# An attention and two-layer feed-forward chain on one core: the tokens of six batches in eight parts of 432 in place of twelve of 288

## The chip, the cores and the metric

The kernel runs on one core of a Trainium2 chip. The metric is the device time of one launch in microseconds (us). Three timed runs of the kernel before gave 1538.23, 1534.93 and 1534.53 us, so a median of 1534.93 us. Durations come from one profiled execution of its own, whose time was 1534.49 us; from its first to its last instruction that execution spans 1532.7 us.

## The reference

For each of 8 batches and 8 heads (576 tokens, 64 dimensions) the memories `phi` (576 x 32) are turned by a softmax over the tokens into weights `a`; `k_m` and `v_m` (32 x 64) are the sums of the keys and the values under these weights. The attention of a token is a softmax over its 32 scores, and its output is `attn @ v_m`:

```python
k_m = np.einsum('bhsm,bhsd->bhmd', a, k)
v_m = np.einsum('bhsm,bhsd->bhmd', a, v)
attn = softmax(q @ k_m.T / 8)
x = concat_heads(attn @ v_m)                  # 4608 x 512
x2 = np.square(np.maximum(x @ w_in, 0)) @ w_out      # 512 -> 2048 -> 512
h = x2 @ w_in2
out = (h - np.tanh(h)) @ w_out2
```

Inputs are drawn as float32; the weights arrive as float64 and are turned into float32 on the chip.

## The kernel before, in words

**Folding.** The first layer never sees `x`. For each batch `v_m` is multiplied into `w_in`: a tile `U` of a batch and a quarter of the hidden features (`fc` = 0 to 3, 512 features) is made by `u_make` (L327): 16 narrow matmuls (L336), two copies on ScalarE (L340) and two subtractions on VectorE (L341), which split U into a high and a low part. `w_in` is kept in memory as `w1_d` and read again for each batch from 2 on (`w1_load`, L190, 1 MB). The softmax over the 32 memories is transposed into `aT` (high and low part) by `att_b` (L360), one generator per half of a batch (288 tokens, `HT`). `att_a` (L217) makes `k_m` and `v_m`, one generator for four heads.

**Layer 1.** A part `u` is one half of a batch, so there are 16 parts (`NU`), and a step is one part and one tile `f` of 128 hidden features, so 256 steps. In a step, `l1_mm1` (L509) makes h by 6 matmuls (L519: three products of high and low, two halves of the 256 contracted rows), `l1_act` (L525) takes relu, square and a high part on ScalarE (L529, L530, L533) and the low part on GpSimd (L534), and `l1_mm2` (L537) adds into four banks of PSUM (512 columns each) by 12 matmuls (L546 to L548). Each of these 18 loads a fresh 128 x 128 weight tile and streams 288 columns. mm1 runs three steps ahead of mm2, act two. After its last step a part goes to memory as `x2_d` by four copies and four stores (`l1_out`, L554).

**Layer 2** (L628 to L698) takes blocks of 512 tokens: 12 matmuls for h, 12 for the output per step, each of 512 columns, 144 steps. Before the end of layer 1 its weights, split by `w2_conv` (L568) during layer 1, are loaded.

**Order.** The program is written out in the order in which generators advance. The opening is the list `ORDER` (L44): every word advances one generator (`i` att_a, `j` att_b, `u` u_make, `w` and `o` the weights' conversion), `S` is a step of layer 1 and `Z` four matmuls of a constant (`warm`, L503, L507; 8 instructions) that give TensorE something to do. A word whose generator is not ready is tried again later. After it, generators are set going at steps that formulas give (L760 to L772), and `tick` (L473) moves each of them by one stage per step when its resources, counted in `free` (L133), are there. Engines work through the program in order, so a matmul that waits holds up all that stand behind it on TensorE; SyncE does the same with the DMA issues.

**Places.** There are four tiles for U (`p_u`), two for `w_in` (`p_w`), two for `aT` (a whole batch each), two for raw weights (`p_raw`), and five of 640 elements in `p_g`; before, one of these five holds the high and the low part of a step (L531).

Of the kernel before, what the change touches and what calls it, by code (L numbers as in the profile page):

```python
# [32 lines left out]
NU = 2 * B  # L33
# [11 lines left out]
w00 w00 i01 w02 w00 w00 w00 o15 w13 o0 o1 w03 i00 i01 w10 w00 o1 w02 w12 w11 o0 Z i00 w03 o1 o1 w31 w11 i01 o0 o0 Z  # L45
i01 Z Z o8 w03 w10 w01 i01 o1 w02 o11 w03 S w10 S u01 w12 u02 j01 w13 Z i00 Z j01 i01 i00 o6 w20 j10 w01 i00 u02 i01
w01 i11 i01 i00 i00 i01 w03 u00 i00 i01 w02 w02 i00 o3 u02 w03 w20 i00 j01 j00 w20 o2 j00 w01 i01 w03 w02 o3 j00 w02
w10 j11 Z u00 w01 w11 u13 o5 o0 o0 w03 w11 w31 i01 u00 o3 j00 i01 o1 i01 o4 i10 u02 o14 w12 S o2 i00 j00 w13 j00 i00
w03 Z o8 j01 j00 j01 o1 j01 o0 o0 w01 o6 w00 j01 j00 Z w02 i00 w02 w02 i01 j00 w13 o3 w12 o2 o3 j00 S w20 o7 Z j01
j11 i10 u10 w32 o3 w33 j01 j00 u01 j01 Z o3 o1 Z i01 j00 Z Z Z o0 S u12 w12 o14 o3 S o0 w12 j01 o4 i00 o4 j00 o2 Z  # L50
w02 o0 o6 i01 w11 w01 o7 o7 o0 u10 j00 i01 j00 j01 w30 Z o5 w23 w02 o5 j10 w00 S w12 Z j00 j01 u03 o0 Z w03 i01 o11
j10 j00 w03 w21 w03 o3 j01 i11 u00 o10 i10 Z w10 w12 u00 w13 Z i00 w12 j01 o6 w11 u01 w03 Z Z o0 i11 i00 i00 w20 j00
j10 w10 j00 u02 w00 w03 i10 u01 o10 Z i11 w23 w13 Z o2 u11 j21 w00 w22 w10 w12 i10 o2 o5 o6 j10 j10 j00 j01 w12 o1
w32 w02 o0 o2 j10 Z w11 j01 u00 u02 o4 j20 w10 w12 o6 u02 w21 w13 w12 j01 o2 w32 i10 j01 i10 S o8 u01 o5 j01 j01 j10
w13 u02 o9 i10 u02 S o5 o1 u01 i10 o10 i10 o3 u02 o5 o1 o5 j01 j01 o1 u00 w12 o7 S o4 j11 o7 j01 i11 u13 j01 j01 u10
u00 u00 S o12 w02 o3 w20 u00 o7 o4 w23 j11 u10 w00 u13 w02 i00 w10 j01 u02 o7 w12 o7 o14 o5 u10 o4 i01 i11 o4 o11 w12
w10 w03 j10 w32 Z w33 j00 j10 w02 i10 o7 i20 u13 o15 w01 o1 i11 w10 o0 u00 u00 o13 i11 o11 w00 o6 o7 o0 w23 w23 i11
o5 o4 o6 o11 o4 i20 w00 o7 j00 j11 o9 o0 j00 w23 o6 w33 w30 o4 S o11 i20 o8 i11 i10 S o4 i01 w10 w21 i11 u03 o10 i11
j10 w10 i00 o3 i10 i11 w10 u02 w21 o6 j11 w20 j00 w11 w11 Z o3 w00 o8 j10 w00 i11 w00 o6 i00 u12 u03 w20 j10 u11 w22
S u13 o0 S j10 u10 j10 j11 o8 o11 S u11 w11 u03 o2 o3 j11 o10 o11 w10 o0 w12 u10 o13 j11 j21 u13 u01 o13 j11 o11 S S  # L60
u11 o8 S o11 w13 j20 j11 j00 w20 u00 u02 S i00 w10 S o13 w03 j11 i20 u11 u00 j11 o5 j11 w10 o7 o11 w20 o3 j20 w02 u00
w21 S o12 o7 i20 w03 o2 j10 o7 w33 w22 o9 j01 i10 u11 o8 u11 j20 S w23 j01 j20 w20 i20 S o11 i20 o2 w33 j20 j01 w00
o14 u02 w30 i20 u01 j21 i00 u10 o8 w32 w22 o9 w31 w31 o2 u02 S u02 i20 j01 w20 i20 w31 w30 S u00 u02 o14 w33 j01 w12
j01 j01 o3 S j01 S u01 w22 w31 o2 i20 u02 w33 w11 o3 o12 w33 w03 u11 w12 w21 w22 j11 j11 w11 o2 u00 w02 j01 w30 w30
w23 j11 j11 j10 j11 j21 o14 o13 o14 w23 S j20 w21 w30 w13 j11 w11 u11 w22 w31 w32 o0 i01 S w22 u12 w33 w33 w13 o5 u03
w00 w01 o11 w00 o4 w02 w21 w12 u00 S u12 w33 j11 w00 i01 w22 u01 w32 w30 w22 o14 u01 j21 j11 j00 o1 i01 u00 w13 w20 S
j21 S o1 o9 o1 w13 S o12 u03 S u10 u10 w13 o0 u10 w23 o14 w22 o9 i10 w22 o10 w22 w11 j11 w22 u12 u03 u12 u00 w20 o9
j21 w22 o13 o13
# [7 lines left out]
def moe_chain_kernel(ctx: ExitStack, tc: tile.TileContext, q, k, v, phi, w1i, w1o, w2i, w2o, out):  # L76
# [52 lines left out]

    def psum(p, name):  # L130
        return p.tile([P, 512], F32, tag=p.name, name=name)

    free = collections.Counter(af=2, b=2, f=3, raw=2, wo=FT, f2=3, kv=1, ph=1, q=1, e=1, vt=2, kt=2, qt=1, sm=1, at=2, w1=2, u=FC)  # L133
# [15 lines left out]
    def conv(src, out, p=None, ahead=1):  # L149
        yield "wo" if p else "raw"  # L150
        raw = slot(p or p_raw, [P, 512, 2], "raw", I32)
# [14 lines left out]
        give("wo" if p else "raw")  # L166
# [50 lines left out]
    def att_a(b, g):  # L217
# [3 lines left out]
        bank, w = (ps_a, "") if own else (ps_b, "b")  # L221

# [35 lines left out]
        for _ in range(4 if b > 2 else 1):  # L258
            yield
# [13 lines left out]
        yield w if own else "b e"  # L273
# [3 lines left out]
        e = e if own else slot(a_e, [P, NC, 4, M], f"e{b}_{g}")  # L277
# [4 lines left out]
        if not own:  # L282
            give("ph")
# [13 lines left out]
        give(*(["u"] * 2 if own else ["kv", "e"]))  # L297
        yield "-"
        n_d = 2 * D if dense else D
# [26 lines left out]

    def u_make(b, fc):  # L327
        yield lambda: {("a", b, g) for g in range(2)} | {("w", fc, pr) for pr in range(4)} <= done and (
            b < 2 or (b, fc) in w1) and (not fc or ("u", b, fc - 1) in done)
        yield "b b u"  # L330
# [7 lines left out]
        u = slot(p_u, [P, 2, 2, 512], f"u{b}_{fc}", F32R)  # L338
# [6 lines left out]
        if b < 2:  # L345
            w1_user(fc)
        else:
            give("w1")
# [6 lines left out]
    at = {}  # L355
# [4 lines left out]
    def att_b(b, r):  # L360
# [11 lines left out]
        elif r == 0:  # L372
            yield "q"
            qs[b] = slot(a_q, [P, 4, 2 * TB, 32], f"q{b}")
            for g in range(2):
                for dh in range(2):
                    src = q[b, 4 * g:4 * g + 4, :, 32 * dh:32 * dh + 32]
                    p0 = 64 * g + 32 * dh
                    nc.sync.dma_start(qs[b][p0:p0 + 32], src.rearrange("i (t p) d -> p i t d", p=32))
            for _ in range(4 if b > 2 else 1):  # L380
                yield
        yield lambda: b in qs
# [20 lines left out]
        yield "sm" if early else "b b" if b == 0 else "b b sm"  # L403
# [5 lines left out]
        give("qt")  # L409
        count(("sc", b), 2, "kt")  # L410
        yield "-"
        if (b, r) == (0, 1):
            s2, a = (slot(p_g, [P, 640], "smx")[:, :2 * HT] for _ in range(2))
        else:
            s2, a = (slot(a_sm, [P, 2 * HT], "sm") for _ in range(2))
# [21 lines left out]
        yield (lambda: b in at) if r else "at"  # L437
        if b not in at:
            at[b] = slot(p_at, [P, 2, 2, 2 * HT], f"aT{b}", F32R)
        hi, lo = (at[b][:, x, :, r * HT:(r + 1) * HT] for x in range(2))  # L440
# [3 lines left out]
        if (b, r) != (0, 1):  # L444
            give("sm")
        done.add(("b", b, r))
# [45 lines left out]
    x2_d = [p_d.tile([ET, P, HT], F32, name=f"x2_d{u}") for u in range(NU)]  # L492
# [16 lines left out]
    def l1_mm1(s):  # L509
# [27 lines left out]
    def l1_mm2(s):  # L537
# [5 lines left out]
        for e in range(ET):  # L543
            o = acc[u][e][:, :HT]
# [9 lines left out]
    def l1_out(u, a):  # L554
        outs = [slot(p_t, [P, HT], "xs") for _ in range(ET)]
        for e in range(ET):
            (nc.vector.tensor_copy if e % 2 and u > 3 else nc.scalar.copy)(outs[e], acc[u][e][:, :HT])  # L557
# [10 lines left out]
    def w2_conv(m, f):  # L568
# [26 lines left out]
    def x2_load(j, c, p_x2f):  # L595
# [8 lines left out]
        while c0 < 512 * (j + 1):  # L604
            u, o = divmod(c0, HT)
            n = min(HT - o, 512 * (j + 1) - c0)
# [153 lines left out]
    for b in range(2, B):  # L760
        s = 32 * (b - 1) - 20
        if b > 2:
            at_step(s, att_a(b, 0))
            at_step(s + 8, att_a(b, 1))
            at_step(s + 10, att_b(b, 0))
            at_step(s + 17, att_b(b, 1))
        for fc in range(FC):
            s0 = (45, 48, 60, 64)[fc] if b == 2 else 32 * (b - 1) + 20 + 4 * fc
            at_step(s0 - 8 if b > 2 else 34 + 2 * fc, w1_load(b, fc))
            at_step(s0, u_make(b, fc))  # L770
    for i in range(2 * FT):
        at_step(40 + 5.3 * i, w2_conv(i % 2, i // 2))  # L772
# [20 lines left out]
    for s in range(next_step[0], N1):  # L793
        if s == N1 - 22:
# [64 lines left out]
```

## Time and profile before

| | before |
|---|---|
| median of 3 runs | 1534.93 us |
| the profiled execution, its own time | 1534.49 us |
| its span | 1532.7 us |
| TensorE matmul busy, share of the span | 99% |
| TensorE weight load busy | 87% |
| VectorE, ScalarE, GpSimd busy | 65%, 55%, 37% |
| matmuls of layer 1's two products | 1536 and 3072 |

Read it so: TensorE's matmul row counts overlapping instructions, so its busy time says only that something is in flight. What a matmul costs is the distance from its start to the start of the next one. PEld is the weight load of TensorE, which runs beside matmuls.

### The profile page before, as it was taken

The page shows a single profiled execution, that of the slowest core. Times are in us where ns is not written, and L with a number is a line of the kernel's source. Part 1 is how long each engine was busy: PE and PEld are TensorE (multiplying, and loading weights), DVE is VectorE, ACT ScalarE, POOL GpSimd, SP SyncE. Part 2 cuts the span into 40 slices and gives each one's busy share as a digit, 9 for nine tenths or more (in the row PEclk, how much of TensorE's full clock was granted, in tenths as well). Part 3 has the DMA queues.
Part 4 walks back from the last instruction along what each step waited for, and adds up shares of the span by engine and source line. Part 5 has one row for each costly group of instructions (what it writes and reads, how often), then busy time and mean ns, then how long its engine had stood idle before and what let it go on. Part 6 is the DMA issues. An engine that isn't in the chain of part 4 may idle for free.

```text
span 1532.7 us, 25852 instructions
## 1 busy us (share of the span) xinstructions
PE 1519.9 (99%) x9880; PEld 1334.2 (87%) x9880; DVE 996.5 (65%) x1385; ACT 845.9 (55%) x1785; POOL 568.1 (37%) x530
## 2 busy tenths in 40 slices
PE   8999999999999999999999999999999999999998
PEld 7988999999899999999988888888888888888887
DVE  5966254545445434410488887878888787888886
ACT  4677676766666666655544444444444444444443
POOL 1565464525344342533442232423333242323322
PEclk7999999999999999999999999999999999999999
DMA  9885575766848383423630001010100101010000
GB/s 296 234 225 157 163 181 129 207 194 185 217 122 249 130 224 133 154 99 130 213 129 17 27 13 44 12 46 11 42 15 0 43 13 44 12 45 11 28 0 28
DMA packets 206907, 161.84 MB, mean 106 GB/s; under 512 B 142656, under 2 KB 182848, under 8 KB 203712
## 3 DMA queue, kind: packets, MB, share of 16 engines
q1 hardware_dynamic: 204336, 157.71, 34.3%
q0 software_dynamic: 2304, 2.36, 1.1%
q8 instruction: 77, 1.26, 0.3%
q14 instruction: 46, 0.38, 0.1%
q10 hardware_dynamic: 144, 0.13, 0.0%
HBM read 117.96 MB, written 42.21 MB: 105 GB/s over the span
## 4 chain that ended last, share of the span: by engine, by line
PE 85%; POOL 0%; ACT 0%; DVE 0%; issue 0%
PE h L637 26%; PE h L519 11%; PE o L683 9%; PE o L682 9%; PE o L681 9%; PE acc L548 7%; PE acc L547 7%; PE acc L546 7%; PE u L336 1%; PE vkm L293 1%; PE sc L408 0%; POOL g L534 0%; PE mb L275 0%; PE vkmT L311 0%; PE m1T L268 0%; ACT sm L427 0%
## 5 line engine op out<-in xcount | busy, mean ns | idle before, releaser
L637 PE MATMUL h<-x,wi 128*128 128x512 f32 x1728 | 414.6, 389 | 0.0
L667 POOL TENSOR_TENSOR gl<-pl,gh 128x512 fp32r<-128x512 f32 x144 | 187.9, 1305 | 535.7 <-PE o L682 512.4
L637 PEld LDWEIGHTS h<-x,wi 128*128 128x128 f32 x1728 | 324.2, 188 | 67.4 <-POOL x L617 0.2
L534 POOL TENSOR_TENSOR g<-gg,g 128x288 fp32r<-128x288 f32 x256 | 227.5, 905 | 358.9 <-ACT g L533 263.7
L649 ACT ACTIVATE u<-h 128x512 f32<-128x512 f32 x144 | 86.1, 598 | 417.5 <-PE h L637 417.5
L548 PE MATMUL acc<-g,wo 128*128 128x288 f32 x1024 | 301.4, 294 | 0.0
L547 PE MATMUL acc<-g,wo 128*128 128x288 f32 x1024 | 301.2, 294 | 0.1
L546 PE MATMUL acc<-g,wo 128*128 128x288 f32 x1024 | 300.6, 294 | 0.0
L519 PE MATMUL h<-aT,u 128*128 128x288 f32 x1536 | 254.2, 301 | 0.5 <-ACT gg L529 0.5
L519 PEld LDWEIGHTS h<-aT,u 128*128 128x128 f32 x1536 | 215.0, 188 | 35.3 <-issue 18.3
L681 PE MATMUL o<-wo,gh 128*128 128x512 f32 x576 | 224.1, 389 | 0.0
L682 PE MATMUL o<-wo,gh 128*128 128x512 f32 x576 | 224.1, 389 | 0.0
L683 PE MATMUL o<-wo,gl 128*128 128x512 f32 x576 | 224.1, 389 | 0.0
L547 PEld LDWEIGHTS acc<-g,wo 128*128 128x128 f32 x1024 | 192.0, 188 | 0.7 <-POOL g L534 0.7
L546 PEld LDWEIGHTS acc<-g,wo 128*128 128x128 f32 x1024 | 192.3, 188 | 0.2 <-ACT xs L557 0.2
L548 PEld LDWEIGHTS acc<-g,wo 128*128 128x128 f32 x1024 | 192.1, 188 | 0.0
L652 DVE SCALAR_TENSOR_TENSOR pl<-u 128x512 f32<-128x512 f32 x144 | 99.5, 691 | 94.5 <-ACT u L649 94.5
L529 ACT ACTIVATE gg<-h 128x288 f32<-128x288 f32 x256 | 104.6, 408 | 91.4 <-PE h L519 82.5
L656 DVE SCALAR_TENSOR_TENSOR pl<-pl,u 128x512 f32<-128x512 f32 x144 | 145.5, 1010 | 0.0
L657 DVE COPY_PREDICATED pl<-m,th 128x512 f32<-128x512 int32 x144 | 140.3, 975 | 4.9
L682 PEld LDWEIGHTS o<-wo,gh 128*128 128x128 f32 x576 | 108.2, 188 | 22.6
L681 PEld LDWEIGHTS o<-wo,gh 128*128 128x128 f32 x576 | 108.0, 188 | 22.5
(107 smaller groups left out, 1873.7 us busy)
## 6 DMA issues: line engine op xcount, KB each, us to landing
w<-w_d SPq DMA_DIRECT2D x24, 1024.0 KB, 6.2
raw<-in_moe_w_in SPq DMA_DIRECT2D x32, 512.0 KB, 6.3
raw<-in_moe_w_out SPq DMA_DIRECT2D x32, 512.0 KB, 5.9
w_d<-w2s SPq DMA_DIRECT2D x32, 512.0 KB, 3.2
q<-in_q SPq DMA_DIRECT2D x32, 288.0 KB, 5.4
x_d<-xs SPq DMA_DIRECT2D x64, 144.0 KB, 2.4
out<-osb SPq DMA_DIRECT2D x17, 512.0 KB, 2.8
wi<-w_d SPq DMA_DIRECT2D x16, 512.0 KB, 6.5
```

The lines of the kernel that those rows point to most:

```text
L519: nc.tensor.matmul(t[:, :HT], uu[:, w, o, c], at[u // 2][:, x, o, u % 2 * HT:u % 2 * HT + HT], start=(n == 0), stop=(n == 5))
L534: nc.gpsimd.tensor_tensor(gl, gg, gh.bitcast(F32), op=ALU.subtract)
L546: nc.tensor.matmul(o, wh[:, c], gh, start=(f == a), stop=False)
L547: nc.tensor.matmul(o, wh[:, c], gl, start=False, stop=False)
L548: nc.tensor.matmul(o, wl[:, c], gh, start=False, stop=(f == z - 1))
L637: nc.tensor.matmul(t, wi[f][:, w, c, :], x, start=(n == 0), stop=(n == 11))
L656: stt(pl, pl, A0, u, op0=ALU.add, op1=ALU.mult)
L657: nc.vector.copy_predicated(pl, m.bitcast(I32), th)
L667: nc.gpsimd.tensor_tensor(lo, pl, hi.bitcast(F32), op=ALU.subtract)
L681: nc.tensor.matmul(o, gh[:, c], wh, start=(f == 0), stop=False)
L682: nc.tensor.matmul(o, gh[:, c], wl, start=False, stop=False)
L683: nc.tensor.matmul(o, gl[:, c], wh, start=False, stop=(f == FT - 1))
```

## The change: what it does, and the diff

Batches 0 and 1 stay in four parts of 288. The tokens of batches 2 to 7 are cut into eight parts of 432, which take three batches at a time: 432 of the first; the last 144 of the first and 288 of the second; 288 of the second and 144 of the third; 432 of the third. Where a part takes in two batches, mm1 runs six matmuls for each piece (144 and 288 columns), into one bank, and needs the U of both batches; mm2 runs 12 matmuls of 432 columns. Layer 1 has 64 + 128 = 192 steps.

U gets six places: four in `p_u`, a new tile `x` that also holds scratch of the first three batches, and one of the two places of `w_in`, from the point where the last U of batch 2 is made (`home`). So `w_in` has one place from then on. `aT` is counted by halves. The high and the low part of a 432-column step take a tile of `p_g` each, two of the five. From batch 2 on `att_a` takes its exponentials in place, and from batch 3 on `att_b` works in the transposed queries' tile. `w2_conv` keeps one raw tile throughout, yields two stages after its load and not three, and issues its store in the stage of the subtraction and not one later. Two clears of `kv_s` go from the start of batch 2 to the end of batch 1. The stages of batches 3 to 7, all U from batch 2 on and `w2_conv` are set going by a table (`PLAN`, 100 items). `ORDER` is another list: 35 steps `S` as before, 20 `Z` and not 28. The loads of layer 2 begin 16 steps before the end of layer 1 and not 22.

```diff
-NU = 2 * B
+WT = 432
+PLAN = """
+c010:68 i60:95 c015:99 j71:58 i40:54 v41:86 j30:22 v61:121 u32:0 v60:106 u40:82 j51:46 c05:74 v30:20 u30:3
...
+    x = slot(p_x, [P, 2048], "x")
...
+    def home(b, fc):
+        if b in (3, 5) and fc < 2 or b in (4, 6) and fc > 1:
+            return "xw"[fc % 2]
+        return "u"
...
-        yield "b b u"
+        yield "b b " + home(b, fc)
...
-            give("w1")
+            give("w" if (b, fc) == (2, FC - 1) else "w1")
...
+    wins = [[(u // 2, u % 2 * HT, HT)] for u in range(4)]
+    for b in range(2, B, 3):
+        wins += [[(b, 0, WT)], [(b, WT, 2 * HT - WT), (b + 1, 0, HT)],
+                 [(b + 1, HT, HT), (b + 2, 0, 2 * HT - WT)], [(b + 2, 2 * HT - WT, WT)]]
...
-        for o in range(2):
-            for w, x in ((0, 0), (0, 1), (1, 0)):
-                nc.tensor.matmul(t[:, :HT], uu[:, w, o, c], at[u // 2][:, x, o, u % 2 * HT:u % 2 * HT + HT], start=(n == 0), stop=(n == 5))
-                n += 1
+        c0 = 0
+        for b, t0, m in wins[u]:
+            n = 0
+            for o in range(2):
+                for w, x in ((0, 0), (0, 1), (1, 0)):
+                    nc.tensor.matmul(t[:, c0:c0 + m], us[b, f // 4][:, w, o, c], at[b % 2][:, x, o, t0:t0 + m], start=(n == 0), stop=(n == 5))
+                    n += 1
+            c0 += m
...
-        g2 = slot(p_g, [P, 2, 320], "g2", F32R)
-        gh, gl = g2[:, 0, :HT], g2[:, 1, :HT]
+        if n == HT:
+            g2 = slot(p_g, [P, 2, HT], "g2", F32R)
+            gh, gl = g2[:, 0], g2[:, 1]
+        else:
+            gh, gl = (slot(p_g, [P, n], "g2", F32R) for _ in range(2))
...
-            o = acc[u][e][:, :HT]
+            o = acc[u][e][:, :wide[u]]
...
         yield from split(x, t[:, 0], t[:, 1], nc.vector)
+        nc.sync.dma_start(w2_d[m, f], t.bitcast(F32))
         give("f")
         yield
-        nc.sync.dma_start(w2_d[m, f], t.bitcast(F32))
...
-        if s == N1 - 22:
+        if s == N1 - 16:
```

## Rows read from the trace of the kernel before

**Rows 1.** The page, part 1, and the granted clock of part 2
```profile
PE 1519.9 (99%) x9880; PEld 1334.2 (87%) x9880; DVE 996.5 (65%) x1385; ACT 845.9 (55%) x1785; POOL 568.1 (37%) x530
...
PEclk7999999999999999999999999999999999999999
```

**Rows 2.** Busy time by stretch: us, PE, PEld, DVE, ACT, POOL, clock, DMA
```profile
0.00:49.18 49.18, 42.41 (x406) 38.09 (x407) 31.17 (x55) 20.96 (x42) 12.03 (x20) 0.83 0.95 299
49.18:100.00 50.82, 50.02 (x485) 44.52 (x483) 40.27 (x56) 35.62 (x85) 27.52 (x27) 1.00 0.77 215
...
135.00:740.00 605.00, 604.61 (x5209) 565.81 (x5209) 243.96 (x372) 406.88 (x945) 260.08 (x284) 1.00 0.57 164
740.00:1532.70 792.70, 788.16 (x3493) 652.98 (x3491) 656.03 (x867) 353.78 (x648) 246.91 (x180) 1.00 0.11 38
```

**Rows 3.** Waits on PE, the longest: us, times, longest
```profile
PE mb L275 <- ACT af L271: 5.2, 2, 4.3
```

**Rows 4.** Timeline of PE, one step of layer 1: start, us
```profile
403.81 0.95 PE L519 MATMUL h<-aT,u 128*128 128x288 f32 x6
404.60 0.29 PE L546 MATMUL acc<-g,wo 128*128 128x288 f32 x1
...
406.18 0.95 PE L519 MATMUL h<-aT,u 128*128 128x288 f32 x6
```

**Rows 5.** Timeline of PE, layer 2
```profile
886.08 0.39 PE L681 MATMUL o<-wo,gh 128*128 128x512 f32 x1
...
888.80 2.88 PE L637 MATMUL h<-x,wi 128*128 128x512 f32 x12
```

**Rows 6.** Groups by line of layer 1: count, busy us, mean ns
```profile
L546 PE MATMUL acc<-g,wo 128*128 128x288 f32 x1024 | 300.6, 294 | 0.0
...
L519 PE MATMUL h<-aT,u 128*128 128x288 f32 x1536 | 254.2, 301 | 0.5 <-ACT gg L529 0.5
```

**Rows 7.** Timeline of PEld, then of PE, around 73 us
```profile
72.42 0.86 PEld L296 LDWEIGHTS vkm<-ones,e 128*128 128x128 f32 x7
73.20 0.84 PEld L519 LDWEIGHTS h<-aT,u 128*128 128x128 f32 x6
...
72.09 1.28 PE L296 MATMUL vkm<-ones,e 128*128 128x1 f32 x10
73.23 1.05 PE L519 MATMUL h<-aT,u 128*128 128x288 f32 x6
```

**Rows 8.** Groups of GpSimd and ScalarE at 288 and 512 columns
```profile
L534 POOL TENSOR_TENSOR g<-gg,g 128x288 fp32r<-128x288 f32 x256 | 227.5, 905 | 358.9 <-ACT g L533 263.7 <-issue 53.2 <-PE acc L548 23.1
...
L667 POOL TENSOR_TENSOR gl<-pl,gh 128x512 fp32r<-128x512 f32 x144 | 187.9, 1305 | 535.7 <-PE o L682 512.4 <-ACT gh L666 16.5 <-ACT x L614 4.4
...
L530 ACT ACTIVATE gg<-gg 128x288 f32<-128x288 f32 x256 | 114.0, 445 | 8.1
L533 ACT CAST g<-gg 128x288 fp32r<-128x288 f32 x256 | 110.9, 433 | 12.9
...
L529 ACT ACTIVATE gg<-h 128x288 f32<-128x288 f32 x256 | 104.6, 408 | 91.4 <-PE h L519 82.5 <-POOL g L534 4.9 <-PE h L507 1.7
...
L649 ACT ACTIVATE u<-h 128x512 f32<-128x512 f32 x144 | 86.1, 598 | 417.5 <-PE h L637 417.5
```

**Rows 9.** DMA issues (KB, us to landing) and SyncE's waits (us, times, longest)
```profile
w<-w_d SPq DMA_DIRECT2D x24, 1024.0 KB, 6.2
...
SPq L579 <- DVE w2s L203: 147.5, 23, 13.6
...
SPq L194 <- PE u L336: 32.9, 4, 12.6
```

**Rows 10.** Timeline of PE before the first step; the constant's matmuls by stretch
```profile
43.80 5.62 PE L507 MATMUL h<-ones 128*128 128x128 f32 x48
49.18 2.61 PE L519 MATMUL h<-aT,u 128*128 128x288 f32 x18
...
0.00:49.18 49.18, 25.74 (x184) 25.04 (x184) 0.83 0.95 299
49.18:100.00 50.82, 5.20 (x43) 4.77 (x41) 1.00 0.77 215
```

More of the change, by code (lines that the diff above doesn't have):

```diff
@@ L50 @@
[L50 to L54, printed above, removed]
@@ L128, in slot @@
         return p.tile(shape, dt, tag=p.name, name=name)
+    x = slot(p_x, [P, 2048], "x")
+    n_e = NC * 4 * M
+    e_x = x[:, :n_e].rearrange("p (c h m) -> p c h m", c=NC, h=4)
+    sm_x = [x[:, n_e + i * 2 * HT:n_e + (i + 1) * 2 * HT] for i in range(2)]
+    at = [slot(p_at, [P, 2, 2, 2 * HT], f"aT{i}", F32R) for i in range(2)]
     def psum(p, name):
         return p.tile([P, 512], F32, tag=p.name, name=name)
-    free = collections.Counter(af=2, b=2, f=3, raw=2, wo=FT, f2=3, kv=1, ph=1, q=1, e=1, vt=2, kt=2, qt=1, sm=1, at=2, w1=2, u=FC)
+    free = collections.Counter(af=2, b=2, f=3, raw=2, wo=FT, f2=3, kv=1, ph=1, q=1, e=1, vt=2, kt=2, qt=1, sm=1, at0=1, at1=1, at2=1, at3=1, w1=2, u=FC, x=0, w=0)
     def give(*rs):
@@ L146, in half, with conv @@
         return slice(64 * o, 64 * o + 64)
[L149 to L151 removed]
+    def conv(src, out, p=None, ahead=1, raw=None):
+        kept = raw is not None
+        if not kept:
+            yield "wo" if p else "raw"
+            raw = slot(p or p_raw, [P, 512, 2], "raw", I32)
         dst = raw.rearrange("p n t -> p (n t)")
@@ L165, in conv @@
         stt(fi, raw[:, :, 0], 29, fi, op0=ALU.logical_shift_right, op1=ALU.bitwise_or)
-        give("wo" if p else "raw")
+        if not kept:
+            give("wo" if p else "raw")
         yield
@@ L257, in att_a @@
             nc.sync.dma_start(x[:NR, :, NC - 1, :D], src[b, heads, n0:].rearrange("h p d -> p h d"))
-        for _ in range(4 if b > 2 else 1):
+        for _ in range(2 if b == 3 else 1):
             yield
@@ L272, in att_a @@
         give_b()
-        yield w if own else "b e"
+        yield w if own else "b" if inplace else "b e"
         t = psum(bank, "mb")
@@ L281, in att_a @@
         give_b()
-        if not own:
+        if not own and not inplace:
             give("ph")
@@ L296, in att_a @@
                 nc.tensor.matmul(vkm[:, 2 * D:2 * D + 1], e[:, c].rearrange("p h m -> p (h m)"), ones[:, :1], start=(c == 0), stop=(c == NC - 1))
-        give(*(["u"] * 2 if own else ["kv", "e"]))
+        give(*(["u"] * 2 if own else ["kv", "ph"] if inplace else ["e"] if (b, g) == (1, 1) else ["kv", "e"]))
+        done.add(("kv", b, g))
         yield "-"
+        if (b, g) == (1, 1):
+            assert ("kv", 1, 0) in done
+            nc.gpsimd.memset(kv_s[:, :, :, :, D:], 1.0)
+            nc.gpsimd.memset(kv_s[NR:, :, :, NC - 1, :], 0.0)
+            give("kv")
         n_d = 2 * D if dense else D
@@ L379, in att_b @@
                     nc.sync.dma_start(qs[b][p0:p0 + 32], src.rearrange("i (t p) d -> p i t d", p=32))
-            for _ in range(4 if b > 2 else 1):
+            for _ in range(2 if b > 2 else 1):
                 yield
-        yield lambda: b in qs
+        yield lambda: b in qs and (b < 3 or ("a", b, 0) in done)
         yield "qt"
@@ L408, in att_b @@
                 nc.tensor.matmul(t[g][p0:p0 + 32, :HT], kt[b][half(g), i], qt[half(g), i, :])
-        give("qt")
+        if b < 3:
+            give("qt")
         count(("sc", b), 2, "kt")
@@ L412, in att_b @@
         if (b, r) == (0, 1):
-            s2, a = (slot(p_g, [P, 640], "smx")[:, :2 * HT] for _ in range(2))
+            s2, a = (slot(p_g, [P, 2 * HT], "smx") for _ in range(2))
+        elif b < 3:
+            s2, a = sm_x
         else:
-            s2, a = (slot(a_sm, [P, 2 * HT], "sm") for _ in range(2))
+            s2, a = (qt[:, 2 * i:2 * i + 2].rearrange("p i n -> p (i n)") for i in range(2))
         s = s2.rearrange("p (t m) -> p t m", m=M)
@@ L436, in att_b @@
         a = a.rearrange("p (g n) -> p g n", g=2)
[L437 to L440, printed above, removed]
+        yield f"at{b % 2 * 2 + r}"
+        hi, lo = (at[b % 2][:, x, :, r * HT:(r + 1) * HT] for x in range(2))
         nc.scalar.copy(hi, a)
@@ L443, in att_b @@
         nc.gpsimd.tensor_tensor(lo, a, hi.bitcast(F32), op=ALU.subtract)
-        if (b, r) != (0, 1):
+        if b > 2:
+            give("qt")
+        elif (b, r) != (0, 1):
             give("sm")
+        if b == 2:
+            count("x", 2, "x")
         done.add(("b", b, r))
@@ L489, in at_step @@
         plan.setdefault(int(s), []).extend(gens)
-    x2_d = [p_d.tile([ET, P, HT], F32, name=f"x2_d{u}") for u in range(NU)]
+    wins = [[(u // 2, u % 2 * HT, HT)] for u in range(4)]
+    for b in range(2, B, 3):
+        wins += [[(b, 0, WT)], [(b, WT, 2 * HT - WT), (b + 1, 0, HT)],
+                 [(b + 1, HT, HT), (b + 2, 0, 2 * HT - WT)], [(b + 2, 2 * HT - WT, WT)]]
+    NU = len(wins)
+    wide = [sum(n for _, _, n in w) for w in wins]
+    start = [sum(wide[:u]) for u in range(NU)]
+    halves = [{(b, r) for b, t0, n in w for r in range(2) if t0 < (r + 1) * HT and t0 + n > r * HT} for w in wins]
+    n_at = collections.Counter(h for hs in halves for h in hs)
+    n_u = collections.Counter(b for w in wins for b, _, _ in w)
+    x2_d = [p_d.tile([ET, P, wide[u]], F32, name=f"x2_d{u}") for u in range(NU)]
     gt, acc = {}, {}
@@ L554, in l1_out @@
     def l1_out(u, a):
-        outs = [slot(p_t, [P, HT], "xs") for _ in range(ET)]
+        outs = [slot(p_t, [P, wide[u]], "xs") for _ in range(ET)]
         for e in range(ET):
-            (nc.vector.tensor_copy if e % 2 and u > 3 else nc.scalar.copy)(outs[e], acc[u][e][:, :HT])
+            (nc.vector.tensor_copy if e % 2 and u > 3 else nc.scalar.copy)(outs[e], acc[u][e][:, :wide[u]])
         yield
@@ L604, in x2_load @@
         while c0 < 512 * (j + 1):
-            u, o = divmod(c0, HT)
-            n = min(HT - o, 512 * (j + 1) - c0)
+            u = max(u for u in range(NU) if start[u] <= c0)
+            o = c0 - start[u]
+            n = min(wide[u] - o, 512 * (j + 1) - c0)
             for i in range(2):
@@ L718, in step_ready @@
             u, f, _, _ = seq[s + 3]
-            if (u // 2, f // 4) not in us or ("b", u // 2, u % 2) not in done:
+            if any((b, f // 4) not in us for b, _, _ in wins[u]) or any(("b", *h) not in done for h in halves[u]):
                 return False
@@ L758, in retry @@
                     k += 1
[L760 to L772, printed above, removed]
+    makers = dict(i=att_a, j=att_b, u=u_make, v=w1_load, c=w2_conv)
+    for item in PLAN.split():
+        name, s = item.split(":")
+        at_step(s, makers[name[0]](int(name[1]), int(name[2:])))
     tile_wise = dict(reuse_waits="tile")
```

85 lines of the change are left out of this document (48 added, 37 removed).

## The prediction

> **What bounds the kernel now.** I read the page first: a matmul is in flight 99% of the span, ScalarE, VectorE and GpSimd are far from full, and the granted clock is 0.9 or more in every slice but the first, the upper of its two levels (2.4 GHz) [rows 1]. The busy time by stretch says where there is room: before the first step of layer 1, at 49.18 us, TensorE is idle or running the constant's matmuls; from 135 to 740 us (layer 1) and to the end (layer 2) it is full [rows 2], and its waits are so few that the longest group of all comes to 5.2 us [rows 3]. So in layer 1 a change is worth what it does to the distances between matmul starts, and these I take from the timeline. Step of layer 1: six of mm1 in 0.79 us and twelve of mm2 in 1.58 us, 131.7 ns for each 288 columns [rows 4]. Layer 2: twelve matmuls of 512 columns in 2.72 us, 226.7 ns [rows 5]. The line through both has 0.424 ns a column and 9.6 ns a matmul. By it 432 columns take 192.8 ns and 144 columns 70.7 ns.
>
> The line holds only while the streaming is the longer half. Every one of these matmuls has its own weight load, and how long the load itself takes is seen where hardly anything is streamed: matmuls with one column have their loads 0.78 us / 7 = 111.4 ns apart, with 128 x 128 weights [rows 7]. The load behind them is that of an mm1 matmul, and its matmul likewise comes no sooner. A matmul of the constant, 128 columns, takes 5.38 us / 48 = 112 ns [rows 10], against 63.9 ns by the line. So about 111 ns is a floor for any matmul with a fresh full tile of weights; 288 columns lie above it, 144 below.
>
> **The change, part by part.**
>
> *mm2 of batches 2 to 7.* Before, 12 parts of 16 steps with 12 matmuls, 2304 of the 3072 [rows 6], x 131.7 ns = 303.4 us; after, 8 parts, 1536 x 192.8 ns = 296.1 us. Gain 7.3 us, all of it on the path, since TensorE is full there.
>
> *mm1 of batches 2 to 7.* Before 12 x 16 x 6 = 1152 of the 1536 [rows 6], x 131.7 ns = 151.7 us. After, three batches take 6 x (432, 144, 288, 288, 144, 432): as many matmuls, as many columns, so by the line nothing changes. But the 144s stand six in a row, 2 x 2 x 16 x 6 = 384 of them. Their ends are 70.7 ns (the load hidden) and 112 ns (the constant's); I take 111.4 ns, the row with the same kind of weights behind it. Sum: 384 x 192.8 + 384 x 131.7 + 384 x 111.4 ns = 74.0 + 50.6 + 42.8 = 167.4 us, a loss of 15.7 us.
>
> The 432 has no row; from the columns at 2.4 GHz the two rows leave 11.7 and 13.4 ns over, so 191.7 to 193.4 ns, which moves the sum by 2 us either way.
>
> The Trainium skill (TensorE: Matmul & The Clock Gate, "LDWEIGHTS") gives a load as columns / 1.2 ns, 106.7 ns for 128; the trace's 111.4 agrees.
>
> *Other engines per step.* By the rows at 288 and 512 columns, ScalarE's three passes come to 530 + 567 + 555 = 1.65 us and GpSimd's to 1.16 us [rows 8], in a step of 18 x 192.8 = 3.47 us, or 3.77 us where a part takes in two batches. Both shares fall. Sixteen copies and sixteen stores of parts fewer: nothing, they lie beside matmuls.
>
> *Five tiles in p_g, two a step.* A new wait: the low part of step s+2 overwrites the high part of s, so GpSimd waits for mm2(s) to end, and behind it on that queue stand att_b's operations and the split of weights. mm2(s+2) wants the low part after mm1, mm2 and mm1, 1.16 + 2.31 + 1.16 = 4.6 us later, and the operation takes 1.16 us: 3.4 us of cover, so nothing. Gone, it would cost up to 1.16 us a step. ScalarE's high part likewise waits for mm2(s-1); behind it are the copies that empty PSUM for U, and the next relu, wanted more than a step later: nothing.
>
> *Six places for U, one for w_in.* The load of w_in for a U cannot start until the U before it has read the place. Its landing takes 6.2 us [rows 9], and a place for U comes free every four steps, so the next U's matmuls stand about three steps, 10.9 us, behind: 4.7 us of cover, counted at nothing. Gone, TensorE stands still at L336 with every matmul behind it.
>
> *Moved stages.* The store of w2_conv goes to SyncE one stage earlier, and that queue already waited for this subtraction 23 times, 147.5 us in all, 13.6 at worst [rows 9]; w_in's loads are behind it. In-place work holds phi's and the queries' tiles longer, and the table sets the stages off elsewhere: the same TensorE work at other steps. The two clears are GpSimd work beside matmuls. Layer 2's loads start 16 x 3.6 = 58 us before the end of layer 1, against 22 x 2.37 = 52. All counted at nothing, behind the fullness of TensorE.
>
> *The opening.* Same 35 steps, eight `Z` fewer: 64 instructions x 112 ns = 7.2 us of TensorE. But 184 of the 224 run before the first step, for 25.7 us [rows 10], in a stretch in which the DMA engines are 0.95 busy [rows 2], so they fill waits and their going gives nothing by itself; those behind it are 5.2 us. No row shows the new order. At most it gains those 25.7 + 5.2 us, and it may lose as much; I take 0, since the same loads have to come first through engines that are full.
>
> **Sum.** -7.3 + 15.7 = +8.4 us on the profiled execution's 1534.5 us: **1542.9 us**. The median of the runs is 0.4 us above that execution.
>
> **The rivals.**
>
> 1. *The short matmuls cost only their columns* (the load of one is under way early enough to hide under two). Then only the gain is left: 1534.5 - 7.3 = 1527.2 us, faster. It decides as soon as the 144s stand less than 70.7 + 7300 / 384 = 89.7 ns apart: from there down the change is a gain. Against it: a load starts only when the matmul before has started [rows 7].
>
> 2. *A load hidden in part.* In a steady row of pairs, load and matmul might overlap better than behind the one-column matmuls. Halfway between the ends, at 91.1 ns, mm1 would lose 7.8 us and the sum be 1535.0 us, no change. Against it: the constant's rows are a steady row of pairs, and stand at 112 ns. The Trainium skill (same page, "Back-to-back issue gap") has 81 ns a matmul for sustained pairs at 128 columns, by which the sum would be 1531.2 us; it also has 131 ns at 512 columns, where the trace has 226.7, so I give it little.
>
> 3. *The opening gives it back.* If the new order starts the first step some 5 us sooner and the eight `Z` had stood on the path, 12 us: 1530.9 us (1527 to 1536). For it: 25.7 us of constants before the first step. Against it: the full DMA engines.
>
> 4. *TensorE waits for U.* Where a w_in load stands behind one of SyncE's mean waits (147.5 / 23 = 6.4 us), its 4.7 us of cover are passed by 1.7 us; behind a long one, by 8.9. Half of some 18 loads at 1.7: 1558 us; more if the long ones meet.
>
> That a part isn't wider than before can't be: 432 columns fit a bank of 512.
>
> **How the numbers follow.** 0.3%, 4.6 us, is about what a measurement of this kernel can tell from no change. Forecast 0.50, with its own range 1537 to 1549 us (432's ends, and the opening by up to 5 us); 0.07 of it lies within 0.3%. Rival 1: 0.12, faster. Rival 2: 0.06, same. Rival 3: 0.22, of which 0.13 faster. Rival 4: 0.10, slower. So faster 0.25, same 0.22, slower 0.53. The range goes from 1526.5 us, rival 1's end, to 1552 us, where a slightly longer opening would put the forecast; rival 4 and the longest gains of 3 are left out.
>
> **What would show it.** mm1 rows of 144 columns about 111 ns apart, six in a row, would show the main term right; some 71 ns would make the prediction wrong, by 15.7 us. mm2 twelve in 2.31 us. A step of 3.47 us for parts of one batch and 3.77 us for the others. The waits of TensorE still a few us in all: L336 waiting for w_in's DMA would be rival 4, mm2 waiting for L534 the five tiles. The first step near 49 us, or rival 3.

## The result, and the profile after

| | median of the runs | ratio to before, 95% interval |
|---|---|---|
| before | 1534.86 us (4 runs) | |
| after | 1549.89 us (1548.34 to 1552.30, 4 runs) | 1.0094 [1.0075, 1.0114] |

The change makes the kernel slower by 0.9%, 15.0 us. The sign and the whole range of the prediction hold; its sum of 1542.9 us is 7 us short, and the median lies 0.9 us above the forecast's own range of 1537 to 1549 us. The profiled execution of after is the longest of its four runs (1552.3 us, span 1550.5 us).

The page of after, parts 1 and 2:

```profile
PE 1528.6 (99%) x9048; PEld 1322.1 (85%) x9048; DVE 984.5 (63%) x1377; ACT 811.6 (52%) x1585; POOL 548.9 (35%) x466
...
PEclk9999999999999999999999999999999999999999
```

TensorE issued 832 matmuls fewer than before [rows 1] (768 of mm2 and 64 of the constant) and was busy longer. A digit 9 stands for 0.9 or more of the upper clock, and the first two slices hide something: the granted clock was 0.50, the lower level, from 16.27 to 23.10 us and from 43.58 to 50.41 us. From there to the end of layer 1 it was 1.00.

From the timeline of TensorE in after (start, us, then engine, line, shape and count), a step of a part that takes in two batches, and mm1 of a part of one batch:

```profile
344.82 0.82 PE L563 MATMUL h<-aT,u 128*128 128x288 f32 x5
345.48 0.36 PE L598 MATMUL acc<-g,wo 128*128 128x432 f32 x1
...
347.84 1.62 PE L563 MATMUL h<-aT,u 128*128 128x144 f32 x12
349.30 0.36 PE L598 MATMUL acc<-g,wo 128*128 128x432 f32 x1
...
494.49 1.34 PE L563 MATMUL h<-aT,u 128*128 128x432 f32 x6
495.66 0.36 PE L598 MATMUL acc<-g,wo 128*128 128x432 f32 x1
```

Twelve of mm2 take 347.84 - 345.48 = 2.36 us, 196.7 ns each. The twelve of mm1 behind them, six of 144 and six of 288 columns shown as one row, take 1.46 us to the next mm2; with 131.7 ns for the 288s [rows 4] the 144s are left with 111.6 ns each. Six of mm1 with 432 columns take 495.66 - 494.49 = 1.17 us, 195 ns each.

The waits of TensorE in after, the first four groups that answer to [rows 3] (us, times, longest):

```profile
PE h L563 <- POOL aT L470: 4.4, 4, 1.4
PE h L563 <- ACT aT L468: 4.3, 1, 4.3
PE u L363 <- DMA w<-w_d: 1.9, 1, 1.9
PE vkm L309 <- ACT att L300: 1.7, 1, 1.7
```

The second and the fourth lie in the opening. The third and two of the four in the first are new and lie among the wide parts: TensorE now waits there for the low part of aT, 1.4 and 1.1 us, and for w_in, 1.9 us, 4.4 us in all.

Where the 17.8 us between the two profiled spans come from can be counted without a remainder, the rounding apart. Step 48 of layer 1 begins at 194.67 us before and 194.96 us after, so the opening and the first 48 steps are worth 0.3 us. From there to the first matmul of layer 2:

| TensorE's time by what was issued (start to next start), us | before | after | difference |
|---|---|---|---|
| mm1 | 169.4 | 64.1 (288) + 79.6 (432) + 43.0 (144) = 186.7 | +17.3 |
| mm2 | 333.1 | 26.1 (288) + 307.6 (432) = 333.7 | +0.6 |
| U and attention | 47.4 | 47.1 | -0.3 |
| sum | 549.9 | 567.5 | +17.6 |

The 384 matmuls of 144 columns take 43.0 us, 112.0 ns each. That mean hides a pattern, which the starts of the single matmuls in the trace show. From the second of a row of six on the distances are 107 to 116 ns. The first is another: where the row stands behind a wide matmul (49 of the 64 rows) the first distance is only 63 to 68 ns, one row with a wait apart; behind the narrow matmuls of U and the attention it is 149 to 174. What is saved behind a wide one is lost again at once: the wide matmul behind the six is 45 ns longer than others of its width (178 and 243 ns in the median at 288 and 432 columns). So a row of six behind a wide matmul still costs six times some 111 ns. Layer 2 is the same within 0.1 us (783.6 and 783.5 us from the start of its first matmul to the end of its last).

### The profile page after: what moved, and what is told of

Its sections match the earlier page's. It is cut to its first block, busy times and chain, and to the rows that moved or that the text cites. A ratio compares the mean times of both kernels' runs of the same rounds, so it can differ in the third digit from the quotient of the medians.

```text
span 1550.5 us, 23737 instructions
## 1 busy us (share of the span) xinstructions
PE 1528.6 (99%) x9048; PEld 1322.1 (85%) x9048; DVE 984.5 (63%) x1377; ACT 811.6 (52%) x1585; POOL 548.9 (35%) x466
## 3 DMA queue, kind: packets, MB, share of 16 engines
q0 software_dynamic: 2304, 2.36, 1.2%
## 4 chain that ended last, share of the span: by engine, by line
PE 93%; DMA 2%; ACT 1%; POOL 1%; SPq 1%; issue 1%; DVE 1%; POOLq 0%; ACTq 0%
PE h L691 25%; PE h L563 14%; PE o L736 8%; PE o L737 8%; PE o L735 8%; PE acc L598 8%; PE acc L599 8%; PE acc L600 8%; PE u L363 2%; PE vkm L309 1%; DMA raw<-in_moe_w_in 1%; PE sc L434 1%; DMA w<-w_d 1%; SPq L271 1%; DMA kv<-in_k 0%
## 5 line engine op out<-in xcount | busy, mean ns | idle before, releaser
L586 POOL TENSOR_TENSOR g<-gg,g 128x432 fp32r<-128x432 f32 (+1 forms) x192 | 208.9, 1095 | 412.7 <-PE acc L599 299.1
L563 PE MATMUL h<-aT,u 128*128 128x288 f32 (+2 forms) x1536 | 262.4, 313 | 10.2 <-POOL aT L470 4.4
L563 PEld LDWEIGHTS h<-aT,u 128*128 128x128 f32 x1536 | 225.5, 191 | 49.8 <-ACT g L585 13.0
L598 PE MATMUL acc<-g,wo 128*128 128x432 f32 (+1 forms) x768 | 260.3, 339 | 0.2 <-ACT xs L609 0.2
L599 PE MATMUL acc<-g,wo 128*128 128x432 f32 (+1 forms) x768 | 259.2, 337 | 0.0
L600 PE MATMUL acc<-g,wo 128*128 128x432 f32 (+1 forms) x768 | 258.8, 337 | 0.1
L585 ACT CAST g<-gg 128x432 fp32r<-128x432 f32 (+1 forms) x192 | 98.5, 513 | 121.4 <-PE acc L600 112.5
L600 PEld LDWEIGHTS acc<-g,wo 128*128 128x128 f32 x768 | 144.6, 188 | 4.2 <-POOL wo L221 0.4
L598 PEld LDWEIGHTS acc<-g,wo 128*128 128x128 f32 x768 | 144.5, 188 | 3.8 <-ACT xs L609 0.4
L599 PEld LDWEIGHTS acc<-g,wo 128*128 128x128 f32 x768 | 144.7, 188 | 3.5
L737 PEld LDWEIGHTS o<-wo,gl 128*128 128x128 f32 x576 | 108.2, 188 | 22.4
L736 PEld LDWEIGHTS o<-wo,gh 128*128 128x128 f32 x576 | 108.1, 188 | 22.5
```

What stands on the lines that cost most here:

```text
L563: nc.tensor.matmul(t[:, c0:c0 + m], us[b, f // 4][:, w, o, c], at[b % 2][:, x, o, t0:t0 + m], start=(n == 0), stop=(n == 5))
L586: nc.gpsimd.tensor_tensor(gl, gg, gh.bitcast(F32), op=ALU.subtract)
L598: nc.tensor.matmul(o, wh[:, c], gh, start=(f == a), stop=False)
L599: nc.tensor.matmul(o, wh[:, c], gl, start=False, stop=False)
L600: nc.tensor.matmul(o, wl[:, c], gh, start=False, stop=(f == z - 1))
L736: nc.tensor.matmul(o, gh[:, c], wl, start=False, stop=False)
```

## The experiments

**1. The distance by width.** Behind the last step of the kernel before:

```diff
+    for n in (64, 128, 144, 192, 208, 224, 240, 256, 272, 288, 320, 352, 384, 416, 432, 448, 480, 512):
+        t = psum(ps_h, "curve")
+        for i in range(24):
+            nc.tensor.matmul(t[:, :n], wi[i % FT][:, 0, i % ET, :], x2[NB - 1, i % ET][0][:, :n], start=(i == 0), stop=(i == 23))
```

> The kernel before, with a block of extra matmuls behind its last step: 24 in a row of each of 18 widths from 64 to 512 columns, each with a fresh 128 x 128 weight tile. Its output is that of the kernel before. Theory (a floor from the weight load): 64, 128, 144, 192, 208 and 224 columns all stand 110 to 113 ns apart, and the distance grows with the columns only from about 240 on. Rival (a fixed part per matmul beside the columns, the load hidden): the distance falls steadily, to about 71 ns at 144 and 37 ns at 64. Second question: 432 columns. By the line of the prediction 192.8 ns; by the changed kernel, whose mm2 rows stand 196 to 197 ns apart in the median, 196 or more, so that the fixed part is not the same at every width.

Measured, first start to last start of a row divided by 23:

```
columns   64     208*   224    240    256    272    288    320    352
ns        108    132    112.0  112.4  119.5  125.4  131.6  146.9  159.9
columns   384    416    432    448    480    512
ns        173.5  188.2  195.2  203.3  216.7  227.7
128, 144, 192 columns: 214 ns at half the clock (below);  * the clock rose inside this row
```

Full-clock neighbours stand 111 to 112 ns apart at 64 columns and 112 to 112.4 in the mean at 224 and 240: a floor, whatever is streamed. (The 108 at 64 columns has in it the first distance of the row, behind a wide matmul, of 28 ns.) From 256 on the columns set the distance. Three widths came out otherwise than either theory had said, and the busy time of the extra block by stretch shows why (us, PE, PEld, granted clock, DMA):

```profile
1526.39:1530.42 4.03, 4.03 (x37) 4.02 (x37) 1.00 0.69 260
1530.42:1544.07 13.65, 13.65 (x66) 13.65 (x66) 0.50 0.00 0
1544.07:1590.00 45.93, 45.93 (x303) 44.87 (x302) 1.00 0.00 1
```

In the second stretch, which begins inside the row of 128 columns and ends inside that of 208, the granted clock is half: 1.2 GHz. The distances there, 213 to 214 ns, are alike for 128, 144 and 192 columns, so the floor is there too, nearly twice as long. In the changed kernel, where only six short matmuls stand together between wide ones, the clock stayed at 1.00 through all wide parts.

The second question is answered as well: 432 columns take 195.2 ns by themselves, not the 192.8 of the line through 288 and 512. The widths from 288 to 480 rise by 0.44 ns a column, and 512 lies below their line (230.9 by it, 227.7 measured), so a line from 288 to 512 comes out too low in between.

**2. Width of the short matmuls in the kernel itself.**

```diff
-nc.tensor.matmul(t[:, c0:c0 + m], us[b, f // 4][:, w, o, c], at[b % 2][:, x, o, t0:t0 + m], ...)
+k, t1 = (224, t0 if c0 else t0 - 80) if m == 144 else (m, t0)
+nc.tensor.matmul(t[:, c0:c0 + k], us[b, f // 4][:, w, o, c], at[b % 2][:, x, o, t1:t1 + k], ...)
```

> The changed kernel with every mm1 matmul of 144 columns widened to 224; the added columns are overwritten by the 288 piece or never read, and where the short piece comes first its 144 columns are those of tokens 80 earlier, so one part in four computes other tokens. Theory (floor from the weight load): 384 matmuls still 111 to 113 ns apart, the whole within 2 us of the changed kernel. Rival (columns count): 384 x 34 ns = 13 us more, 1563 us.

1553.82 us, ratio 1.0125 [1.0109, 1.0142]; the interval overlaps that of after. The groups of mm1 from step 48 on in this run (count, busy us, mean ns of one, idle before):

```profile
L564 PE MATMUL h<-aT,u 128*128 128x288 f32 x458 | 75.8, 300 | 0.0
L564 PE MATMUL h<-aT,u 128*128 128x224 f32 x384 | 54.4, 277 | 1.4 <-POOL aT L470 1.4
```

and in after:

```profile
L563 PE MATMUL h<-aT,u 128*128 128x288 f32 x458 | 76.8, 302 | 0.0
L563 PE MATMUL h<-aT,u 128*128 128x144 f32 x384 | 52.1, 271 | 1.4 <-POOL aT L470 1.4
```

More than half as many columns again move the mean time in flight of one matmul from 271 to 277 ns and the median distance not at all (111 ns in both). The first distance of a row behind a wide matmul does follow the columns (102 ns and not 66 in the median), and the wide matmul behind the row gives it back: six short matmuls and the wide one behind them take 843 ns in the mean in both runs, the row with the wait left out. From step 48 to layer 2 the runs take 567.8 and 567.5 us. So the columns of a short matmul cost nothing here. That it is the load of a full weight tile, and not a price of every matmul, fits two things: the loads of such a row stand 108 to 113 ns apart themselves in both runs, and the attention's matmuls with weights of 32 columns (L309) stand 31 ns apart in the mean over that stretch. The median of the runs is 3.9 us up, more than the 2 us expected; the traces can't say why, since the two profiled executions, the shortest of four here and the longest of four in after, both took 1552.3 us.

**3. No short matmuls.** In a part of two batches mm1 runs six matmuls of 432 columns from one batch:

```diff
         for b, t0, m in wins[u]:
+            if len(wins[u]) > 1:
+                c0, m, t0 = 0, (0 if m < HT else WT), t0 // 2
             n = 0
-            for o in range(2):
+            for o in range(2 if m else 0):
```

> The changed kernel with mm1 of the parts that take in two batches as six matmuls of 432 columns from one batch in place of six of 144 and six of 288; it leaves out the other batch's tokens there (a quarter of the tokens of batches 2 to 7 are those of the wrong batch), everything else stays: places, waits, table, mm2. Theory (the short matmuls at the floor of the weight load are what makes the change a loss): 64 steps x 6 x (112 + 132 - 196) ns = 18.4 us less than the changed kernel, 1529 to 1535 us, so no slower than before. Rival (the loss is in the waits for places and w_in): 1545 us or more.

1543.22 us, 1.0044 [1.0030, 1.0057]. Neither end: 6.7 us came back, not 18.4. The waits of TensorE say where part of the rest stayed:

```profile
PE h L565 <- POOL aT L470: 7.4, 5, 2.3
...
PE u L363 <- DMA w<-w_d: 4.2, 1, 4.2
```

With shorter steps the low part of aT and w_in come late more often: among the wide parts the waits come to 9.9 us, against 4.4 in after. The clock took another part: during or right behind three of these waits the granted clock fell to 0.50, from 319.6, 531.3 and 585.9 us on, for 13.7 us in all, in which a matmul of 432 columns took up to 360 ns and not 197. From step 48 to layer 2 this run takes 561.4 us, 6.1 less than after. The timeline of GpSimd in after shows why the first is late:

```profile
360.62 1.12 POOL L586 TENSOR_TENSOR g<-gg,g 128x432 fp32r<-128x432 f32 x1 [1.57 <-PE acc L599]
364.52 1.12 POOL L586 TENSOR_TENSOR g<-gg,g 128x432 fp32r<-128x432 f32 x1 [2.79 <-PE acc L599]
365.59 1.40 POOL L470 TENSOR_TENSOR aT<-qt,aT 128x576 fp32r<-128x576 f32 x1
```

L470 had its input from ScalarE some 3.4 us earlier (L468 ran from 361.52 to 362.18 us), but GpSimd stood at L586, which waits for mm2: the step's two parts take two of the five tiles. TensorE, in turn, waited for L470 until 367.05 us. That wait at L586 comes to 299.1 us in 110 times over the run; before, the wait for mm2 was 23.1 us [rows 8].

**4. The low part of aT on VectorE,** alone and together with experiment 3:

```diff
-        nc.gpsimd.tensor_tensor(lo, a, hi.bitcast(F32), op=ALU.subtract)
+        (nc.vector if b > 2 else nc.gpsimd).tensor_tensor(lo, a, hi.bitcast(F32), op=ALU.subtract)
```

> The changed kernel with the low part of aT of batches 3 to 7 made on VectorE, not GpSimd. Theory (with two tiles of p_g a step GpSimd's queue stands behind mm2, so this low part comes late, and TensorE waited for it twice in steady state, 1.5 us each): those two waits go, 1545.5 to 1548 us. Rival (TensorE then waits for what stands behind it): 1549 to 1552 us.

1549.17 us, 1.0081 [1.0068, 1.0095]. The median is the rival's number; but the kernel before took 1.2 us longer in the runs beside it, and 1.0081 of 1534.86 us is 1547.3 us, the theory's. The interval overlaps that of after, so the times don't decide. The two waits are gone from the trace, and from step 48 to layer 2 the run takes 566.4 us, 1.1 us less than after; a wait for w_in of 2.3 us stays, and behind it the granted clock is 0.50 for 3.4 us, which after did not have. In the changed kernel as it is, GpSimd's queue is worth 1 to 3 us.

> Both edits at once: the changed kernel without the short matmuls (1543.2 us, whose trace has TensorE waiting 7.4 us for the low part of aT and 4.2 us for w_in) and with that low part made on VectorE. It leaves out the same tokens as the run without the short matmuls. Theory (the rest of that run's missing gain sits in GpSimd's queue, which stands behind mm2): these waits go, 1536 to 1540 us. Rival (TensorE then waits for the next late thing, U behind its one place for w_in): 1541 to 1545 us.

1533.05 us, 0.9981 [0.9970, 0.9992]: the theory's side, 3 us below its range. The waits of TensorE:

```profile
PE u L363 <- DMA w<-w_d: 5.2, 2, 4.4
PE h L565 <- ACT aT L468: 4.3, 1, 4.3
PE vkm L309 <- ACT att L300: 1.7, 1, 1.7
PE h L565 <- POOL aT L470: 1.7, 2, 0.9
```

Between the last two kernels only the short matmuls differ (and, with them, that a step reads the U and aT of one batch and not of two), 1549.17 and 1533.05 us, 16.1 us (by the ratios, 0.0100 of 1535 us, 15.4 us). From step 48 to layer 2 it is 566.4 and 551.7 us, 14.7 us. Counted from the distances it is 64 x 6 x (112 + 132 - 196) ns = 18.4 us; the longer wait for w_in takes about 3 of it. So once the queue behind them is out of the way, the short matmuls are the whole loss of the change, within the 2 us by which that stretch is longer than before (549.9 us). The pair also shows what experiment 3 lacked: 9.7 us, of which 4.7 are waits, and most of the rest is 13.7 us at the lower clock against 3.4.

**5. Parts of 288 in the changed kernel.**

```diff
-    for b in range(2, B, 3):
-        wins += [[(b, 0, WT)], ...
+    wins += [[(b, r * HT, HT)] for b in range(2, B) for r in range(2)]
...
+        s = int(s) if int(s) < 64 else 64 + 1.5 * (int(s) - 64)
         at_step(s, makers[name[0]](int(name[1]), int(name[2:])))
...
-        if s == N1 - 16:
+        if s == N1 - 22:
```

> The changed kernel with all six batches in twelve parts of 288 again, its six places for U, its one place for w_in, its opening and its table (whose steps after 64 are stretched by 1.5). Theory (the loss is in the cut into 432 and 144 + 288): about 15 us less than the changed kernel, 1533 to 1537 us, the same as before. Rival (the loss is in the places, the table and the waits that they bring): 1544 us or more.

A miss: 1574.56 us, 1.0262 [1.0244, 1.0279]. mm1 and mm2 stand 133 ns apart in the median as before, but TensorE waits:

```profile
PE u L363 <- DMA w<-w_d: 15.2, 6, 9.6
PE sc L434 <- DVE qt L412: 6.7, 1, 6.7
```

With steps of 2.37 us, places for U come free every four steps, 9.5 us, and not every 14, and the load through the one place for w_in is late six times, by 9.6 us at worst. After the two longest waits, or during them, the granted clock is 0.50 for 6.8 and 13.7 us. The run doesn't isolate the cut, as I had meant it to; that the one place and the table live off the longer steps is how I read it, and the next run tests part of that.

**6. Four places for U, two for w_in and the formulas of before, with parts of 288.**

```diff
-        if b in (3, 5) and fc < 2 or b in (4, 6) and fc > 1:
-            return "xw"[fc % 2]
...
-            give("w" if (b, fc) == (2, FC - 1) else "w1")
+            give("w1")
...
-    makers = dict(i=att_a, j=att_b, u=u_make, v=w1_load, c=w2_conv)
-    for item in PLAN.split():
...
+    for b in range(2, B):
+        s = 32 * (b - 1) - 20
...
+    for i in range(2 * FT):
+        at_step(40 + 5.3 * i, w2_conv(i % 2, i // 2))
```

> The run with parts of 288 in the changed kernel (1574.6 us), now with four places for U, two for w_in and the formulas of before for the stages; the new opening, the in-place attention stages, the one raw tile of w2_conv stay. Theory (that run lost its time to the one place for w_in and to the table, which was made for other parts): 1531 to 1538 us. Rival (in-place stages or w2_conv's one tile hold TensorE up): 1545 us or more.

A second miss, on the rival's side: 1599.42 us, 1.0409 [1.0394, 1.0423]. The waits for w_in are gone; once a batch mm1 stands for some 7 us, the first time 13.2. Around these waits the granted clock is 0.50 for 51.2 us between step 48 and layer 2. That stretch takes 614.7 us and not 549.9: 48.1 of the 64.8 us are waits of TensorE, and the lower clock can account for most of the rest. The waits of TensorE, and the timeline of ScalarE at one of them:

```profile
PE h L559 <- ACT gg L574: 50.2, 8, 13.2
```
```profile
310.66 0.66 ACT L177 ACTIVATE wf<-raw 128x512 f32<-128x512 f32 x1 [10.79 <-DMA raw<-in_moe_w_out]
311.22 0.40 ACT L574 ACTIVATE gg<-h 128x288 f32<-128x288 f32 x1
```

ScalarE stood 10.8 us at w2_conv's conversion, whose raw weights had not landed, and the relu that empties mm1's bank is behind it in the queue. The chain of that stretch leads through that load, issued at 306.12 us, back to SyncE at the keys of the next batch. w2_conv now yields two stages after its load and not three, and I take that to be too few where SyncE is held up; whether three would have done was not tried.

**7. The opening lists exchanged.** The kernel before with the list of after, and after with the list of before (in each, `ORDER` alone is replaced).

> The kernel before with the opening list of the changed kernel and nothing else of it. Theory (the new list starts layer 1 some 6 us earlier and loses it again by step 48, as the traces of both kernels show, since the loads set the pace): within 3 us of before, 1532 to 1538 us. Rival (the list is a gain that the changed kernel's tighter places eat up): 1528 to 1530 us.

1532.85 us over ten runs, 0.9988 [0.9978, 0.9998]. The first step of layer 1 begins at 43.09 us and not 49.18, step 48 at 193.95 us and not 194.67: of 6.1 us, 0.7 are left. This is the one complete kernel here that is at least as fast as both; its interval ends 0.02% short of no change. Where the lead goes is seen in both kernels with this list. In after:

```profile
37.91 1.16 PE L549 MATMUL h<-ones 128*128 128x128 f32 x8
43.35 0.44 PE L563 MATMUL h<-aT,u 128*128 128x288 f32 x1 [4.28 <-ACT aT L468]
44.83 5.81 PE L563 MATMUL h<-aT,u 128*128 128x288 f32 x23 [1.04 <-POOL aT L470]
50.48 0.29 PE L598 MATMUL acc<-g,wo 128*128 128x288 f32 x1
```

The kernel before ran 48 of the constant's matmuls right up to its first step [rows 10], with a granted clock of 1.00. With the new list TensorE stands still there for 4.3 us, and the clock is 0.50 for 6.8 us (from 43.58 us in after, from 43.11 in this run). The 23 matmuls from 44.83 us take 5.65 us, 246 ns each: 2.6 us more than at 131.7 ns. TensorE's waits between the first step and step 48 come to 4.9 us in this run and 1.1 before.

> The changed kernel with the opening list of before. Theory (both lists are paced by the same loads; what one gains before the first step it loses by step 48): within 3 us of the changed kernel, 1547 to 1553 us. Rival (the new list hides part of the change's loss): 1555 us or more.

A miss, on the rival's side: 1592.81 us, 1.0371 [1.0357, 1.0385]. Step 48 comes at 196.2 us, 1.2 us later than in after; the loss lies between there and step 64, which begins at 276.5 us and not 243.0. The list also moves the attention of batch 2, and TensorE waits for one attention stage after the other, 18.6 us in that stretch (in after, none). The longest, from the timeline:

```profile
247.10 1.57 PE L435 MATMUL sc<-qt,kt 64*32 64x288 f32 x16 [2.01 <-DVE x L448]
...
256.64 1.21 PE L435 MATMUL sc<-qt,kt 64*32 64x288 f32 x16 [7.97 <-DVE qt L413]
...
261.70 0.73 PE L564 MATMUL h<-aT,u 128*128 128x432 f32 x1 [3.85 <-ACT aT L469]
```

The clock fell with it: from 235.19 to 269.32 us, 34.1 us, it was 0.50, which can account for most of the other 14 us of this stretch. That the stages come one after the other because they now share the tile `x` and the queries' tile is how I read it; no run takes the sharing away. The two parts of the change, list and places, can't be taken apart in that direction.

## Why the prediction was right, and where it was not

*mm1, a loss of 15.7 us.* Right: +17.3 us measured. The 144s take 112.0 ns each, where the row of one-column matmuls [rows 7] had given 111.4, and the run with 224 columns shows that their columns don't matter. The agreement of the sum is closer than that of its parts: the two waits for aT (2.9 us by the distances) and the 432s at 196 ns (1.2 us) add 4.1 us that the sum did not have, and mm1's distances where it follows other work came out about 2.5 us shorter.

*mm2, a gain of 7.3 us.* This step failed. Measured: +0.6 us. The sum took 192.8 ns for 432 columns, from a line through 288 and 512, with ends of 191.7 and 193.4; the distance is 195.2 ns by itself and 196 in steady state, outside those ends. At 196, 1536 matmuls take 301.1 us, 5 us more than the sum had. The remaining 3 us are mainly the wait for w_in, 2 us, and the 45 ns more of the first matmul behind 32 rows of short ones, 1.5 us. Per column, 432 (0.454 ns) is hardly better than 288 (0.457); 512 (0.443) is.

*Rivals 1 and 2* (short matmuls at the price of their columns, or in between): no, by the distances in after and by experiments 1 and 2. Once per row of six a distance is as short as rival 1 had it (66 ns, behind a wide matmul), but the wide matmul behind the row pays for that. The 81 ns a matmul that the Trainium skill gives for sustained pairs at 128 columns (TensorE: Matmul & The Clock Gate, "Back-to-back issue gap") are not reached here: no row of experiment 1, down to 64 columns, averages under 108 ns.

*The opening, 0.* The number is right: the new list starts layer 1 6 us earlier and has lost that by step 48, in after as in experiment 7. Rival 3 expected it to be kept; the sign named for it, a first step well before 49 us, came without it. The reason given, the loads that have to come first, is not shown to be the one: 2.6 us went to the lower clock behind 4.3 us in which TensorE stood still, where before the constants had run, and 3.8 us to more waits, none of them put down to a DMA. So the constants do not only fill waits: with the new list, which has fewer of them, TensorE stood still at that place and the clock fell. That the list would fit either set of places was not in the prediction, but was my theory in experiment 7, and was wrong.

*Covers counted at nothing.* ScalarE's held. The 3.4 us for GpSimd's low part held too, but I priced only that operation and not the one behind it: the new wait on GpSimd's queue makes aT's low part late twice, by 1.4 and 1.1 us. The 4.7 us of cover for w_in were passed once, by 1.9 us. So rival 4 came true in kind, at 1.9 us in this execution, 4.4 with the waits for aT, not at 15.

*Put together:* 15.7 - 7.3 became 17.3 + 0.6, with the waits inside. The measured loss is nearly twice the sum. That 1549.9 us still lies inside the range is luck: the room above 1549 us had been left for a longer opening, and it was mm2's missing gain that used it.

## What to carry to other kernels

In a row of matmuls, each with a fresh 128 x 128 weight tile in these types, one cost 111 ns at the upper clock however few columns it streamed, so a cut that makes parts wider must be counted with the narrow pieces that it leaves at its seams. Here the pieces cost some 17 us, and the wide parts gave next to nothing for them. Take the price of a new width from a row of that width, or measure it, before a saving of a few per cent per matmul is built on a line through two others. When an operation gets a new wait, price what stands behind it on its queue, not only the operation. And look at the granted clock of the stretch before all of a loss is put down to waits: in six of the runs here a stretch at the lower clock came with the longest waits and made them dearer.

## What the runs showed of the hardware that I had not expected

TensorE's clock fell once although the engine never idled: in experiment 1 the granted clock was 0.50, the lower level of 1.2 GHz, for 13.65 us, from the row of 128 columns to that of 208, and each matmul then took 213 to 214 ns; the matmuls before (1.00 of the clock) had been of 512 columns, then of 64 and of 128. It is one execution, and what brought the clock down is not shown. Narrow matmuls alone don't always do it: in the kernel before, 48 of 128 columns stand in a row from 43.80 to 49.18 us, 112 ns apart [rows 10], at a granted clock of 1.00.

Elsewhere it fell during or right behind waits of TensorE: 4.3 us in the opening with the new list, 13.2 us and some 7 us in experiment 6. A wait alone does not settle it: one of 3.7 us in the second run of experiment 7 left it at 1.00.

A row of short matmuls is paid for at its end and not at its start. The first distance behind a wide matmul is about the columns' time (28 ns at 64 columns, 66 at 144, 102 at 224), the next ones are the floor, and the wide matmul that follows is longer by what the first one saved.

The distance is not one fixed part plus the columns: beyond the number of columns divided by 2.4 GHz it is, in experiment 1, 11.6 ns at 288, 13.5 at 384, 15.2 at 432, 16.7 at 480 and 14.4 at 512.
